# Fused memory-attention and gated feed-forward block on one core: an earlier first weight load, a reordered first copy, and a new table of priorities

## The chip, the cores and the metric

The kernel runs on one core of one Trainium2 chip. A core has five engines with a queue of their own each: TensorE (PE, matrix products into PSUM), VectorE (DVE), ScalarE (ACT), GpSimd (POOL) and SyncE (SP), which here issues every DMA transfer. The metric is the device time of one execution in microseconds, as the median of several runs.

## What is computed

The input is x, 2048 tokens by 1024 features in bf16. The reference computes

```
h   = x + A(layernorm(x))          # 32 heads of 32, four segments of 512 tokens
out = h + (silu(n @ w1) * (n @ w3)) @ w2     with n = layernorm(h), 3584 hidden features
```

A projects the normalised tokens with wq, wk and wv. In each of the four segments it runs causal softmax attention inside the segment, and adds what a running memory of the earlier segments returns for phi(q), mixed by a gate per head; the result is multiplied with wo. The change concerns the order of work only; what is computed stays as it is.

## The kernel before

**How it is built.** The Python program does not write the instruction streams by hand. Each step is an operation in a graph with its allowed engines, an estimated cost, what it reads and writes, a class `cls` and a sequence number. `Graph.schedule` then plays the graph through with these estimates: whenever an engine is free, it takes the ready operation with the lowest (class, sequence number). The order that comes out per engine is emitted, with semaphore waits for the dependences. So the order within each engine's queue is fixed before the program runs; if an estimate is off, the engine waits at that place for the real event, with everything behind it in the queue.

**The table SHIFT.** Operations are numbered in units (`stage()` starts a new one: one projection, one group of scores, one layer norm, one copy). For a unit that is in the table, `schedule` adds the first number to its sequence number and the second to its class:

```
late, cls = SHIFT.get(o.unit, (0, 0))
o.seq += late + 1e-6 * o.seq
o.cls += cls
```

The table therefore only says which of several ready operations goes first. It adds and removes no operation.

**The stages.** A layer norm and the q, k and v projections of a segment feed that segment's attention. In attention, for each of eight pairs of segment and half of the heads, there are ten groups of scores (line 1101, four PSUM banks each), each followed by an exponential on ACT (L1115) and a causal mask on POOL (L1124); then one long visit of products in columns of 32 (L1194 and its neighbours L1187 and L1029) for numerators, denominators and the memory. For segments 1 to 3 a visit that retrieves the memory (L1316) comes later. The denominators' reciprocals are spread over rows; for segments 2 and 3 this goes through DRAM: a store to `r_scr`, then eight loads with repetition (L1281) into `R0w` and `R1`. Between the visits the scheduler puts pieces of dense 128x128 products (all at L747): the next segment's projections, the product with wo, and, near the end, the first feed-forward products with w1 and w3. After about 400 us only the feed-forward part is left.

**The start.** `first_half` issues the loads in one queue: token tiles x0, x1, x2, then the first half of the first query weights (256 columns), tile x3, the first half of the key weights, and the remaining weights. The fourth item of each load is a scale for its estimated transfer time; it changes the schedule only. `first_tile` normalises tile t in place: statistics (tiles 0 and 2 on DVE, L874, L877, L900; tiles 1 and 3 on ACT, L860, L863), the power -1/2 on POOL (L901), two multiplications of 512 columns on DVE (L905), eight transposes on PE (L759) and two copies out of PSUM into `xnT`, each on DVE (L771) or ACT (L770), whichever the scheduler finds free. Statistics on DVE of tile 2 depend on `self.applied[0]`, the first multiplication of tile 0. The first projections (q and k, features 0 to 255) then run in pieces of 128 tokens, as soon as each tile is there.

Of the kernel before, what the change touches and what calls it, by code (L numbers as in the profile page):

```python
# [30 lines left out]
    0: (-18, 0), 3: (-173, 0), 4: (-182, 0), 5: (1074, 0), 6: (1041, 1), 7: (-959, -1),  # L31
    8: (-283, 1), 9: (1560, 1), 10: (-14, 0), 11: (1, 0), 12: (51, -1), 13: (-257, 0),
    14: (-1703, 0), 15: (2952, 0), 16: (-2912, 0), 18: (-87, -1), 19: (3455, 1), 20: (-401, -1),
    21: (22, 0), 22: (2924, -1), 23: (-669, 0), 24: (-328, -1), 26: (-261, -1), 27: (11, -1),
    28: (-153, 0), 29: (-317, 0), 31: (1524, -1), 32: (211, 0), 33: (-1, 0), 34: (2, 0),
    35: (-15, 0), 38: (118, 1), 39: (2057, 0), 40: (223, 0), 41: (2279, -1), 42: (914, 1),
    43: (-1135, 1), 44: (2665, 1), 45: (3218, 1), 47: (1997, 1), 48: (664, -1), 49: (1928, -1),
    50: (-2800, -1), 51: (7, 0), 52: (-1130, 0), 53: (116, 0), 54: (669, 0), 55: (1018, 0),
    56: (2, 0), 57: (-289, 1), 58: (4, 0), 59: (731, 0), 60: (-304, 0), 61: (-436, 0),
    62: (64, 1), 63: (-3, 0), 64: (-63, 0), 65: (-50, 0), 66: (-174, 0), 67: (-937, 0),  # L40
    68: (808, 0), 69: (1512, -1), 70: (28, 0), 71: (-58, 1), 72: (1441, 1), 73: (-75, 1),
    74: (2141, 0), 75: (778, 1), 76: (-752, 1), 77: (90, 1), 78: (-21, 0), 79: (151, 0),
    80: (1343, 0), 81: (-1130, 0), 83: (160, 0), 84: (687, 0), 85: (-676, 0), 86: (312, 0),
    87: (-266, 0), 88: (-263, 0), 89: (-1189, -1), 90: (-164, 0), 91: (680, 1), 92: (-1801, 0),
    93: (1499, 0), 94: (3153, 0), 95: (-261, 0), 96: (0, -1), 97: (-11, 0), 98: (2, 0),
    99: (944, 0), 100: (-54, 0), 101: (1016, 0), 102: (-842, 0), 103: (147, 0), 104: (-1191, 0),
    106: (-47, 0), 107: (121, 1), 108: (-1142, 0), 109: (-1295, -1), 111: (699, 0),
    112: (-365, -1), 113: (-594, 0), 115: (28, 0), 116: (2452, -1), 117: (-8, 0), 118: (676, 0),
    119: (54, 0), 120: (-1449, -1), 121: (235, 0), 122: (-9, -1), 123: (-13, 1), 124: (45, 0),
    125: (-1279, 1), 127: (-283, -1), 129: (555, 0), 130: (1438, -1), 132: (617, 1),  # L50
    133: (81, 0), 134: (-2285, -1), 135: (-179, 0), 136: (3199, 1), 137: (389, 0),
    138: (920, 0), 139: (146, 1), 140: (687, 1), 141: (27, 0), 142: (-619, 1), 143: (1934, 1),
    144: (-922, 0), 145: (415, -1), 146: (-312, 0), 147: (-26, 0), 148: (-870, 0),
    149: (2501, 1), 150: (1682, 0), 151: (-28, 0), 152: (609, 1), 153: (611, 0), 154: (-302, 0),
    156: (0, 1), 157: (-185, 1), 158: (391, 0), 159: (-373, 0), 160: (-610, 0), 161: (-1748, 0),
    162: (-133, 0), 163: (-4056, 1), 164: (1073, 1), 166: (-202, 0), 168: (-3204, -1),
    169: (-2075, -1), 170: (2581, -1), 171: (-39, 1), 172: (-122, 1), 173: (-18, 1),
    174: (-37, 0), 175: (34, 0), 176: (1853, 1), 177: (-140, 0), 178: (-301, 0), 179: (204, 0),
    181: (165, 0), 182: (-13, 0), 183: (-7, 0), 184: (687, -1), 185: (-271, 0), 186: (-861, 1),
    187: (-616, 1), 188: (355, -1), 189: (-1449, 1), 190: (1132, 0), 191: (114, 0),  # L60
    192: (-22, 0), 193: (-464, 0), 194: (-2, 0), 195: (294, 0), 196: (18, 0), 197: (-2089, 0),
    199: (-2443, 0), 200: (248, -1), 201: (1, 0), 203: (210, 1), 204: (-1070, 0), 206: (-70, 0),
    207: (1441, 0), 208: (525, 0), 209: (839, 0), 210: (10, 0), 211: (-262, 0), 212: (894, -1),
    213: (203, 1), 214: (-359, 1), 215: (-2, 0), 216: (696, -1), 217: (-735, 0), 218: (-51, 0),
    219: (4750, 0), 220: (-465, -1), 221: (-23, 0), 222: (-196, 1), 223: (399, 0),
    224: (-1932, 1), 225: (-192, 0), 226: (-134, 0), 227: (-1542, 1), 229: (153, 1),
    230: (-676, 1), 231: (-73, 0), 232: (618, 1), 234: (-465, 0), 235: (0, -1), 237: (222, -1),
    238: (609, 0), 239: (1282, 0), 241: (-183, 1), 242: (845, 1), 243: (811, -1),
    244: (1681, -1), 246: (6, 1), 248: (-2423, -1), 249: (11, 0), 250: (21, 0), 251: (-2902, 1),
    252: (-599, 1), 253: (927, 0), 255: (308, -1), 256: (4, -1), 257: (-382, 0), 258: (30, 0),  # L70
    259: (-35, 0), 260: (-73, -1), 261: (-386, 0), 262: (-58, 1), 263: (-1713, 0),
    264: (-165, 0), 265: (-369, 1), 266: (-12, 0), 267: (808, -1), 268: (1356, 0),
    269: (-538, 0), 270: (576, -1), 272: (27, 0), 273: (609, 0), 275: (-27, 0), 277: (0, -1),
    279: (-4, 0), 280: (-3, 0), 281: (176, 0), 282: (-28, -1), 284: (-175, -1),
    285: (-1255, -1), 286: (-196, 0), 287: (308, 0), 288: (1028, 0), 289: (-18, 0),
    290: (-217, -1), 291: (628, 0), 292: (21, 0), 293: (11, 0), 294: (1042, 0), 295: (6, 0),
    296: (150, -1), 297: (222, 0), 298: (1329, 0), 299: (-799, 0), 300: (-3, 0), 301: (303, -1),
    302: (-473, -1), 303: (2419, -1), 304: (528, 0), 305: (-99, 0), 306: (2531, -1),
    307: (-28, 0), 309: (-1338, 1), 310: (-4, 1), 311: (836, 0), 312: (-154, 0), 315: (-261, 0),
    316: (443, 0), 317: (-31, -1), 318: (-1464, -1), 319: (-220, 0), 320: (340, 0),  # L80
    321: (1268, 0), 322: (-21, -1), 323: (-2755, 1), 324: (-54, 0), 325: (1643, -1),
    326: (-57, 0), 327: (1851, 0), 328: (-2912, 0), 329: (317, 1), 330: (-690, 0),
    331: (-712, -1), 332: (-940, 0), 333: (-1099, 1), 334: (-615, 1), 335: (-16, 0),
    336: (496, 0), 337: (664, 0), 338: (-166, 0), 339: (-46, 0), 340: (-700, 0), 341: (-385, 1),
    342: (-1713, 0), 344: (51, 0), 345: (-756, -1), 346: (178, -1), 348: (803, 0),
    350: (1942, -1), 351: (169, 0), 352: (-492, 1), 354: (14, 0), 355: (-39, 0), 356: (290, 0),
    357: (99, 0), 358: (-389, 0), 359: (1761, 0), 361: (1409, 0), 362: (-58, -1), 363: (550, 1),
    364: (-95, 1), 365: (-140, 1), 366: (56, 1), 367: (-11, 1), 368: (-1627, 0),
    369: (-393, -1), 370: (-2089, 0), 372: (27, 0), 373: (204, -1), 374: (-55, 0),
    375: (-622, 0), 376: (-1005, -1), 377: (-179, 0), 378: (-1188, 1), 379: (1478, -1),  # L90
    380: (-865, -1), 381: (-543, 0), 382: (-70, 0), 383: (-64, 0), 384: (-1160, 0),
    385: (-2800, 0), 386: (0, 1), 387: (-193, 1), 388: (-133, 0), 390: (2419, 0),
    391: (2201, -1), 392: (-35, -1), 394: (45, -1), 395: (-2041, 0), 396: (410, 0),
    397: (571, 1), 399: (-543, -1), 400: (-965, 0), 401: (2531, 0), 402: (-462, -1),
    403: (-129, 0), 404: (-89, 1), 405: (-60, -1), 407: (-887, 1), 408: (3072, 0),
    409: (3013, 0), 410: (1761, 1), 411: (1584, 0), 413: (281, 1), 414: (562, 0),
    415: (-1293, -1), 416: (1707, 0), 417: (-995, -1), 418: (1637, 0), 419: (-785, -1),
    420: (3, 0), 422: (-913, -1), 423: (-121, -1), 424: (-7, 0), 426: (-2, 0), 427: (-1, 0),
    430: (-1, 0), 431: (14, 0), 432: (8, 0), 433: (-33, 0), 435: (-1086, 0), 436: (72, 0),
    437: (51, -1), 438: (-293, -1), 439: (37, 1), 440: (1527, 1), 441: (-212, 0),  # L100
    442: (-3190, 1), 443: (-1357, -1), 444: (-520, 1), 445: (904, 0), 446: (-1018, -1),
    447: (697, 0), 449: (2458, 0), 450: (-40, 0), 451: (-44, 0), 452: (-8, 0), 453: (-14, 0),
    454: (658, -1), 455: (-3, 0), 456: (1, 0), 457: (-3, 0), 459: (-2315, 1), 461: (-1, 0),
    462: (539, 0), 463: (66, 0), 464: (788, 1), 465: (29, 0), 466: (24, 0), 467: (2995, 0),
    468: (-306, 1), 469: (310, 0), 470: (-30, -1), 471: (-796, 0), 472: (-70, 1),
    473: (3455, 1), 474: (62, -1), 475: (-550, 0), 476: (-2089, 0), 477: (2158, 0),
    478: (-306, 1), 479: (4, 0), 480: (1506, -1), 481: (-470, -1), 482: (3857, 0),
# [500 lines left out]
class Kernel:  # L608
# [283 lines left out]
    def first_tile(self, t):  # L892

        x = self.xs[t][:, :]
# [8 lines left out]
        for b in range(2):  # L903
# [4 lines left out]
            gr = Group([(0,), (1,), (2,)], safe=True)  # L908
# [53 lines left out]
    def first_half(self):  # L962
# [16 lines left out]
        x = self.xnT[0]  # L979
# [531 lines left out]
```

The softmax here doesn't subtract the row's maximum and nothing guards it: scores larger than these inputs give would overflow.

## Time and profile before

| what | value |
|---|---|
| median of 3 runs | 888.77 us (888.38 to 888.92) |
| profiled execution | span 886.3 us |
| TensorE clock granted | 1.0 |
| busy: DVE, ACT, POOL | 449.2, 302.5, 178.4 us |
| HBM read, written | 84.94 MB, 9.44 MB |

In 40 slices the page shows where each engine is busy, in tenths of the slice (22 us each):

```profile
PE   9999999999999999999999999999999999999998
DVE  6697878786665797645545301323243333341011
ACT  5878675779645555511111000101011111110000
```

Read it as three stretches: the start, in which TensorE has little to do for some 8 us; attention with dense work between its visits up to about slice 17; and the feed-forward part, in which DVE and ACT have little to do. Matmuls are pipelined and the profile models their ends, so a 9 for PE does not say that no time is lost between them. The page's groups show the three largest rows, out and in by name, count, busy time and mean duration of one, and idle time before them:

```profile
L747 PE MATMUL ps<-hnT,w1b 128*128 128x512 bf16 x875 | 219.8, 379 | 2.0 <-issue 0.5
L747 PE MATMUL ps<-hnT,w3b 128*128 128x512 bf16 x879 | 217.1, 379 | 1.5 <-issue 0.5
L747 PE MATMUL ps<-w2b,hm 128*128 128x512 bf16 (+2 forms) x935 | 198.5, 366 | 0.9
```

### The profile page before, as it was taken

Reading aid. Unit: us, or ns where it says so; the run is one execution under the profiler, and the core shown is the slowest. Engines: PE = TensorE matmul, PEld = TensorE weight load, DVE = VectorE, ACT = ScalarE, POOL = GpSimd, SP = SyncE. Lnnn points to the kernel's source line nnn. Section 1 sums busy time; section 2 is a strip of 40 time slices with the busy share of each in tenths; the row PEclk is TensorE's granted clock in tenths of the full one; section 3 lists DMA queues with packets and bytes.
Section 4 is the critical chain, followed back from the end, with each engine's and each line's share of the span. In section 5 each row is a group of like instructions: output and inputs, shape, how many; then the busy total and the mean of one; then the engine's idle time right before and its main releaser. Section 6 shows DMA issues by size and latency. Waiting matters only on the chain.

```text
span 886.3 us, 13649 instructions
## 1 busy us (share of the span) xinstructions
PE 873.0 (99%) x5732; PEld 400.5 (45%) x5821; DVE 449.2 (51%) x699; ACT 302.5 (34%) x345; POOL 178.4 (20%) x226
## 2 busy tenths in 40 slices
PE   9999999999999999999999999999999999999998
PEld 5444444444444344444444444444444444444445
DVE  6697878786665797645545301323243333341011
ACT  5878675779645555511111000101011111110000
POOL 2544443455252455303000000000000000000000
PEclk9999999999999999999999999999999999999999
DMA  7869939464862736198354410221323321301010
GB/s 238 208 185 244 227 91 267 125 156 119 217 155 74 175 83 156 53 300 258 103 156 107 120 35 30 78 65 54 83 61 88 95 72 48 90 7 41 30 54 24
DMA packets 148796, 105.75 MB, mean 119 GB/s; under 512 B 46336, under 2 KB 134400, under 8 KB 147712
## 3 DMA queue, kind: packets, MB, share of 16 engines
q1 hardware_dynamic: 148736, 104.89, 44.5%
q8 instruction: 46, 0.75, 0.4%
q14 instruction: 14, 0.11, 0.0%
HBM read 84.94 MB, written 9.44 MB: 106 GB/s over the span
## 4 chain that ended last, share of the span: by engine, by line
PE 94%; DMA 2%; DVE 2%; issue 1%; POOL 0%; ACT 0%; SPq 0%; ACTq 0%; POOLq 0%; DVEq 0%
PE ps L747 88%; PE ps L1194 3%; PE ps L1101 3%; DMA R0w<-r_scr 1%; DMA r_scr<-T 1%; DVE oT L1332 0%; SPq L1281 0%; DMA xs<-in_A_x_dram 0%; PE ps L1029 0%; DVE lnst L874 0%; ACT et L1115 0%; PE ps L1316 0%; POOL et L1124 0%; DVE hm L1397 0%; PE ps L1187 0%
## 5 line engine op out<-in xcount | busy, mean ns | idle before, releaser
L747 PE MATMUL ps<-hnT,w1b 128*128 128x512 bf16 x875 | 219.8, 379 | 2.0 <-issue 0.5
L747 PE MATMUL ps<-hnT,w3b 128*128 128x512 bf16 x879 | 217.1, 379 | 1.5 <-issue 0.5
L747 PE MATMUL ps<-w2b,hm 128*128 128x512 bf16 (+2 forms) x935 | 198.5, 366 | 0.9
L1389 ACT ACTIVATE sg<-ps 128x512 bf16<-128x512 f32 x112 | 66.8, 597 | 385.9 <-PE ps L747 385.8
L1392 DVE SCALAR_TENSOR_TENSOR t<-sg,ps 128x512 bf16<-128x512 bf16 x112 | 76.7, 685 | 183.1 <-ACT sg L1389 182.6
L1115 ACT ACTIVATE et<-ps 128x2048 bf16<-128x2048 f32 x80 | 150.0, 1874 | 45.1 <-PE ps L1101 44.7
L747 PEld LDWEIGHTS ps<-w2b,hm 128*128 128x128 bf16 x952 | 90.9, 98 | 103.0
L747 PEld LDWEIGHTS ps<-hnT,w1b 128*128 128x128 bf16 x896 | 86.2, 98 | 106.3 <-issue 6.5
L747 PEld LDWEIGHTS ps<-hnT,w3b 128*128 128x128 bf16 x896 | 86.3, 98 | 106.1 <-issue 3.6
L1124 POOL TENSOR_SCALAR_AFFINE_SELECT et<-et 128x512 bf16<-128x512 bf16 (+1 forms) x96 | 93.1, 976 | 133.0 <-ACT et L1115 132.7
L1397 DVE SCALAR_TENSOR_TENSOR hm<-t,ps 128x512 bf16<-128x512 bf16 x112 | 76.2, 685 | 40.8 <-PE ps L747 39.0
L1421 DVE TENSOR_TENSOR ob<-hr,ps 128x512 bf16<-128x512 bf16 (+2 forms) x34 | 22.2, 655 | 120.6 <-PE ps L747 120.4
L747 PE MATMUL ps<-wo,oT 128*128 128x512 bf16 x246 | 60.9, 379 | 1.1 <-issue 0.8
L747 PE MATMUL ps<-xnT,wp 128*128 128x512 bf16 (+1 forms) x345 | 59.6, 320 | 1.3 <-issue 0.8
L747 PE MATMUL ps<-hnT,wp 128*128 128x512 bf16 x249 | 59.4, 380 | 0.8 <-issue 0.6
L1138 DVE TENSOR_TENSOR sum<-sum,et 128x512 bf16<-128x512 bf16 (+1 forms) x64 | 43.6, 684 | 11.6 <-POOL et L1124 6.1
L747 PEld LDWEIGHTS ps<-xnT,wp 128*128 128x128 bf16 x352 | 28.0, 98 | 26.9 <-issue 2.8
L747 PEld LDWEIGHTS ps<-wo,oT 128*128 128x128 bf16 x256 | 23.9, 98 | 29.9 <-issue 3.3
L747 PEld LDWEIGHTS ps<-hnT,wp 128*128 128x128 bf16 x256 | 23.5, 98 | 29.7 <-issue 3.9
L1101 PE MATMUL ps<-qT,kT 32*128 32x128 bf16 (+3 forms) x512 | 31.7, 301 | 0.0
L747 PE MATMUL ps<-wp,xnT 128*128 128x512 bf16 x123 | 30.2, 379 | 0.4 <-issue 0.2
L747 PE MATMUL ps<-wp,hnT 128*128 128x512 bf16 x123 | 29.6, 380 | 0.5 <-issue 0.3
(97 smaller groups left out, 560.1 us busy)
## 6 DMA issues: line engine op xcount, KB each, us to landing
w3b<-in_B_w_dram SPq DMA_DIRECT2D x28, 512.0 KB, 4.1
w1b<-in_B_w_dram SPq DMA_DIRECT2D x28, 512.0 KB, 4.0
wp<-in_A_wv_dram SPq DMA_DIRECT2D x8, 1024.0 KB, 6.5
wp<-in_A_wq_dram SPq DMA_DIRECT2D x7, 1024.0 KB, 5.6
wp<-in_A_wk_dram SPq DMA_DIRECT2D x7, 1024.0 KB, 7.2
w2b<-in_B_w_dram SPq DMA_DIRECT2D x7, 1024.0 KB, 5.8
xs<-in_A_x_dram SPq DMA_DIRECT2D x16, 256.0 KB, 5.9
h<-in_A_x_dram SPq DMA_DIRECT2D x16, 256.0 KB, 4.0
```

The source lines that it names most:

```text
L747: return [e.matmul(p[0](gr), p[1], p[2], start=p[3], stop=p[4]) for p in part]
L1101: ins.append(e.matmul(self.bank(gr, j, 512 - 128 * kc, off), k[r, g0 + g, 128 * kc:128 * kc + 128], q[r, g0 + g, 128 * kc:512], start=True ...
L1115: return [e.activation(et[:, :, :], src, AF.Exp, scale=self.scale)]
L1124: self.pool_op(lambda e, v=v, pat=pat: e.affine_select(v, v, pattern=pat, compare_op=ALU.is_ge, fill=0.0, base=0, channel_multiplier=-1), ...
L1138: lambda e, gr: [e.tensor_tensor(out, x, y, op=ALU.add)], reads=[x, y],
L1194: ins.append(e.matmul(self.ps[32 * i:32 * i + 32, b * 512 + c0:b * 512 + c0 + n], lhsT(i, kc, j), rhs(i, j), start=kc == 0 and j == first, ...
L1389: self.g.op("act", act_ns(512), lambda e, gr, sg=sg: [e.activation(sg, self.bank(gr), AF.Tanh, scale=0.5)], writes=[sg], cls=0, group=gg)
L1392: e.scalar_tensor_tensor(t1, sg, 1.0, self.bank(gr), op0=ALU.add, op1=ALU.mult)], reads=[sg], writes=[t1], cls=0,
L1397: e.scalar_tensor_tensor(dst, t1, 0.5, self.bank(gr), op0=ALU.mult, op1=ALU.mult)], reads=[t1], writes=[dst], cls=0,
L1421: self.g.op("dve", dve_ns(n), lambda e, gr, hs=hs, ob=ob, n=n: [e.tensor_tensor(ob, hs, self.bank(gr, 0, n), op=ALU.add)], reads=[hs], wri ...
```

## The change

Three edits. In the queue of loads, the first query weights go ahead of the third token tile x2, and the scales of these two loads are set anew. In `first_tile`, the first of the two copies of tile 0 may only run on DVE, and the statistics of tile 2 depend on that copy in place of the first multiplication, so that they come behind it. And the table SHIFT is replaced as a whole: nearly every entry has other numbers. The aim is that the first projection finds its weights and its tokens sooner, and that the rest of the schedule fits the new start.

```diff
 SHIFT = {
-    0: (-18, 0), 3: (-173, 0), 4: (-182, 0), 5: (1074, 0), 6: (1041, 1), 7: (-959, -1),
...
+    0: (-7, 0), 3: (38, 0), 4: (2985, 0), 5: (497, 1), 6: (310, 0), 7: (-6129, 0), 8: (-30, 1),
...
         var, mean, op = self.ln_act(t, x) if t % 2 else self.ln_stats(
-            t, x, 1, (self.applied[0],) if t else ())
+            t, x, 1, (self.copied,) if t else ())
...
-            self.evac(gr, out, 512, lambda v: v[:, 0:512].rearrange("p (k n) -> p k n", k=4),
-                      cls=1, bf=True, engs=("dve", "act"))
+            o = self.evac(gr, out, 512, lambda v: v[:, 0:512].rearrange("p (k n) -> p k n", k=4),
+                          cls=1, bf=True, engs=("dve", "act") if t or b else ("dve",))
+            if t == 0 and not b:
+                self.copied = o
...
-        loads = [x[0] + (1.04,), x[1] + (0.7,), x[2] + (1.2,),
-                 (wq[:, :, 0:256], sq[:, :, 0:256], 1.54), x[3] + (0.65,),
+        loads = [x[0] + (1.04,), x[1] + (0.7,), (wq[:, :, 0:256], sq[:, :, 0:256], 1.3),
+                 x[2] + (1.0,), x[3] + (0.65,),
                  (wk[:, :, 0:256], sk[:, :, 0:256], 0.74),
```

## The prediction

> **What bounds the kernel now.** I read the page's engine shares and its chain first, then the chain in order of time for the start, the timeline there, the waits of TensorE, and last a count of TensorE's visits. The page first:
>
> ```profile
> PE 873.0 (99%) x5732; PEld 400.5 (45%) x5821; DVE 449.2 (51%) x699; ACT 302.5 (34%) x345; POOL 178.4 (20%) x226
> ...
> PE 94%; DMA 2%; DVE 2%; issue 1%; POOL 0%; ACT 0%; SPq 0%; ACTq 0%; POOLq 0%; DVEq 0%
> ```
>
> TensorE is on 94% of the chain that ended last. The 99% alone prove little: one 512-column matmul is shown with 379 ns, but two that follow each other start 216 ns apart. So I counted weight loads between changes of kind in the trace. A dense stretch takes 216 ns for each load plus about 0.11 us: the chain below has 12 matmuls in 2.70 us, and 12 x 0.216 = 2.59. From the first projection to the end, TensorE makes 80 visits for scores, 8 for the columns, 6 for the retrieval and 4 groups of transposes, with a dense stretch between any two. The scores' visits take 0.33 us. Hardly a stretch is longer than its count. The exceptions in all of attention add up to 2.2 us: 0.9 at 298 us (the retrieval waits for rows of R), 0.5 at 309 (DVE hm), 0.35 at 266 (ACT sg), 0.3 at 175 (a mask) and 0.1 at 258. The view of TensorE's waits names the same places, with smaller sums because it counts from modelled ends:
>
> ```profile
> PE ps L1316 <- DMA R<-r_scr: 0.8, 1, 0.8
> PE ps L747 <- DVE hm L1397: 0.4, 1, 0.4
> PE ps L747 <- ACT xnT L770: 0.3, 1, 0.3
> PE ps L747 <- ACT sg L1389: 0.3, 1, 0.3
> ```
>
> So three things are left to win: these 2.2 us, the start, and the number of visits. The chain of the start, in order of time (start, duration, what):
>
> ```profile
> 6.07 0.47 DVE xs L905 x2
> 6.54 0.18 issue
> 6.72 0.69 DVE lnst L874
> 7.41 0.32 DVE xnT L771
> 7.73 0.30 DVE lnst L874
> 8.03 0.22 issue
> 8.25 0.72 DVE xs L905 x2
> ...
> 9.66 1.07 PE ps L747 x16
> 10.73 0.45 PE ps L759 x8
> 11.18 2.23 PE ps L747 x40
> 13.41 0.45 PE ps L759 x8
> 13.86 2.68 PE ps L747 x48
> ...
> 20.34 2.70 PE ps L747 x12
> ```
>
> VectorE leads until 9.66 us, TensorE from there without a gap: 40 small matmuls in 2.23 us are 56 ns each, the pitch at which they start one after another. The timeline shows what the first projection waits for:
>
> ```profile
> 7.05 0.60 ACT L770 ACTIVATE xnT<-ps 128x512 bf16<-128x512 bf16 x1
> 7.32 0.41 DVE L771 COPY xnT<-ps 128x512 bf16<-128x512 bf16 x1
> 7.76 0.68 PEld L747 LDWEIGHTS ps<-xnT,wp 128*128 128x128 bf16 x12 [0.62 <-DMA wp<-in_A_wq_dram]
> ```
>
> The copy by ACT ends at 7.65, and the weights, issued at 2.18 with 5.1 us to landing, are there at about 7.3. Both come close together, and the copy is the later.
>
> [...] x3, issued at 2.66, lands after 5.4 us at 8.1, and the key weights, issued at 3.81, after 6.7 us at 10.5. I use it for one thing: exchanging two loads leaves what lies behind both where it was.
>
> **The loads.** Before, x2 lands at about 5.6 us and wq at 7.3, in the trace's landing events. Exchanged, wq comes 256 KB earlier. x1 landed at 4.3, and wq took 7.3 - 5.6 = 1.7 us behind x2, so I expect it at 4.3 + 1.7 = 6.0 to 6.4; x2 then lands at about 7.3. x3 (8.1) and the key weights (10.5) have the same bytes ahead of them and stay.
>
> **The copy.** The first four transposes are done when ACT starts at 7.05. DVE needs 0.41 in place of 0.60, so the copy ends at 7.46 and the first projection starts at about 7.58 instead of 7.79: 0.2 us earlier. The second half goes to ACT (7.32 to about 7.92) or DVE (to 7.87). The eight matmuls on the first half last 8 x 56 ns = 0.45, to 8.03, so it is nearly in time: cost 0 to 0.1.
>
> **What queues behind the new wait.** On DVE, in order, behind the copy: the statistics of tile 2 (two of 0.69), the multiplications of tile 1 (0.72, ready at 7.94 when POOL ends), and the copies of tile 1. If the multiplications go first, they start at 7.97 and not 8.25, 0.3 earlier. If both statistics go first, they start at 7.46 + 2 x 0.69 = 8.84, 0.6 later. Tile 2 itself becomes ready 0.6 to 1.1 us later than its 10.67.
>
> **What reaches the end of the start.** Nothing, most likely. The key weights can be used from 10.5 to 10.6 us. At 10.57 TensorE has, before, just finished all it can do without key weights and tile 2: q for tiles 0 and 1. From there 96 matmuls and 16 transposes are left, 112 x 56 ns = 6.3 us, without a gap to 16.6. After the change the same work is left at the same time, since only tile 2 could be taken ahead and it comes later, not sooner. Its delay is hidden too: k for tiles 0 and 1 is 32 x 56 ns = 1.8 us, to 12.4, and tile 2 is multiplied by 11.8 at the latest. I take 0 for the start; the ends are -0.3 (if a few transposes slip in ahead) and +0.5 (if statistics go first, or a k matmul stands in the queue ahead of its weights).
>
> **The new table.** It adds no work. It can shift waits, and visits. The visits are forced: a score group needs four banks which ACT frees 1.88 us after the last one, so dense work has to lie between, and the columns and retrievals hold the same banks. 98 visits stay 98. What is left is the 2.2 us of waits. Nothing in the profile says that new priorities miss more or less often in the small; the largest wait, 0.9, is one of four retrievals fed through DRAM, of which the other three wait for nothing. I take 0.6 in its place: 2.2 becomes 1.9, from 0 to 6. That is the largest unknown. The scheduler's rate and fixed time for a load (260 bytes per ns and 1.9 us) give 2.9 us for the 256 KB store into r_scr; the chain at 286 us has 5.39. So the late retrievals are planned with a time that is too short, by luck of the table with slack or without. Sum: 0 for the start, -0.3 for waits: 888.77 - 0.3 = 888.5.
>
> **The rivals.** *Waits vanish.* All 2.2 us go, the start gives 0.1 to 0.3: 888.77 - 2.3 = 886.5 at the very best, typically 886.8. For it: TensorE needs nothing new, the five waits are separate, and the dense work is there to fill them. Against: the long ones depend on transfers whose time the schedule does not know. *A staged transfer is missed,* which ends slower. The loads of L1281 land in 3.2, 6.6 (median) and 10.1 us. A retrieval ordered for the median waits 10.1 - 6.6 = 3.5 us when it meets weight traffic, with all dense products queued behind it. There are four such retrievals, in segments 2 and 3; now one of them waits 0.9. One full miss gives 888.5 + 3.5 = 892.0, a partial one of 2 us or a few small ones 890.6 to 891. *The start turns against itself:* DVE takes both statistics first, and TensorE idles 0.5 us, 889.2. For it: tile 2's statistics are no longer done when tile 1 is ready. Against: the slack before the key weights.
>
> **How the numbers follow.** Likeliest, 50%: start hidden, waits of the same size, 888.5. Waits vanish, 20%: 886.8. A staged transfer missed, 22%: 891. Start against itself, 8%: 889.2. The bound of 0.2% is 1.8 us, so 887.0 and 890.5 are the limits: faster 0.2, same 0.58, slower 0.22. The range leaves out about half of each outer case: below 886.7 only nearly everything at once would do, above 891.3 a full miss.
>
> **What would show it.** The start: the first projection at about 7.6, but the first score visit still at 17.3 within 0.4. If it comes at 16.9 or earlier, the key weights landed sooner than I say, and my step on the loads is wrong. The visits: dense stretches of 216 ns per load plus 0.11, and 98 visits. The waits: the view of TensorE's waits with one to three entries of under 1 us. An entry of over 2 us at L1316 would be the staged transfer. If the time falls below 886.5, there was something left that my count of stretches did not see.

## The result, and the profile after

| | median us | range | ratio to before, 95% interval |
|---|---|---|---|
| before, beside it | 888.58 | 887.82 to 888.92 | |
| changed | 895.15 | 894.57 to 896.89 | 1.0078 (1.0061 to 1.0096) |

The change costs 6.6 us; the prediction said 888.5, with 891.3 as its upper end. The profiled execution of the changed kernel is its slowest, 896.89 us with a span of 895.2; the others are 1.2 to 2.3 us faster, and one reason for that comes out below. Line numbers in the changed kernel are 3 lower up to about L900 and 1 lower after it (L747 is L744, L1316 is L1315, L1281 is L1280). In most experiments the code is some 90 lines longer, so L744 is L834 to L839 there.

The page of the changed kernel, engine shares and chain:

```profile
PE 882.0 (99%) x5821; PEld 401.8 (45%) x5821; DVE 447.3 (50%) x699; ACT 301.5 (34%) x341; POOL 187.0 (21%) x230
...
PE 91%; DMA 5%; SPq 1%; DVE 1%; ACT 0%; issue 0%; POOL 0%; DVEq 0%
```

The busy shares have hardly moved: TensorE is at 99% as before. The chain has: TensorE fell from 94% to 91%, and transfers rose from 2% to 5%. The view of TensorE's waits names the places (engine, tile, line, releaser; then total us, times, longest):

```profile
PE ps L756 <- DVE xs L902: 2.3, 2, 1.3
PE ps L1315 <- DMA R<-r_scr: 1.6, 1, 1.6
PE ps L1028 <- issue: 1.3, 1, 1.3
PE ps L744 <- DVE oT L809: 1.2, 1, 1.2
PE ps L744 <- DMA h<-in_A_x_dram: 1.2, 1, 1.2
PE ps L1100 <- DVE R L1328: 0.9, 1, 0.9
PE ps L744 <- DMA w1b<-in_B_w_dram: 0.6, 1, 0.6
```

The idle 1.2 us ahead of the very first matmul (L809 here) were there before too. Beside them the kernel before had no wait with a named releaser over 0.8 us (under "issue", without a releaser, it had 3.7 us in 23 pieces of at most 0.2; its profile lacks the records of 89 of its 5821 matmuls). Now there are six entries from 0.6 to 2.3. To see where they lie I used the count of the prediction: the time from one kind of TensorE work to the next, less 0.216 us for each dense load (0.056 for each small piece), 0.106 for each return to dense work, 0.33 for a score visit, and for a column visit its columns at the pace of the dense loads, four products side by side (512 columns in 0.216 us; in the kernel before, four products of 256 columns start 0.11 us ahead of the next four). What is left, in us:

| stretch, us (rounded) | before | changed |
|---|---|---|
| start, to 22 | 0.6 | 3.7 |
| 22 to 170 | 1.1 | 1.6 |
| 170 to 245 | 1.1 | 2.2 |
| 245 to 262 | 0.1 | 1.5 |
| 262 to 330 | 2.3 | 2.7 |
| 330 to 375 | 0.1 | 1.6 |
| from 375 | 0.0 | 0.8 |
| sum | 5.2 | 14.1 |

The sums differ by 8.9 us, as the spans do (895.2 - 886.3): the loss is idle or slow time of TensorE, and two thirds of it lie behind the start. Of the 3.7 us at the start, 1.7 are lost to half clock, which only some executions have (below); in part that is why this slowest execution loses more than the 6.6 us of the medians. Dense stretches are 100 and column visits 10, against 98 and 8 before: the new order takes the first segment's columns in three parts.

### The profile page after: what moved, and what is told of

It reads as the page before. It is cut to its first block, busy times and chain, and to the rows that moved or that the text cites. A ratio compares the mean times of both kernels' runs of the same rounds, so it can differ in the third digit from the quotient of the medians.

```text
span 895.2 us, 13715 instructions
## 1 busy us (share of the span) xinstructions
PE 882.0 (99%) x5821; PEld 401.8 (45%) x5821; DVE 447.3 (50%) x699; ACT 301.5 (34%) x341; POOL 187.0 (21%) x230
## 4 chain that ended last, share of the span: by engine, by line
PE 91%; DMA 5%; SPq 1%; DVE 1%; ACT 0%; issue 0%; POOL 0%; DVEq 0%
PE ps L744 85%; PE ps L1193 3%; PE ps L1100 3%; DMA R0w<-r_scr 1%; DMA R<-r_scr 1%; DMA h<-in_A_x_dram 1%; DMA wp<-in_A_wk_dram 1%; SPq L1280 1%; DMA w1b<-in_B_w_dram 1%; ACT et L1114 0%; DMA r_scr<-T 0%; SPq L319 0%; POOL et L1123 0%; PE ps L1028 0%; DVE R L1328 0%
## 5 line engine op out<-in xcount | busy, mean ns | idle before, releaser
L744 PE MATMUL ps<-hnT,w1b 128*128 128x512 bf16 x896 | 221.4, 379 | 0.9 <-DMA w1b<-in_B_w_dram 0.6
L744 PE MATMUL ps<-hnT,w3b 128*128 128x512 bf16 x896 | 218.2, 379 | 0.0
L744 PE MATMUL ps<-w2b,hm 128*128 128x512 bf16 (+2 forms) x952 | 200.2, 366 | 0.0
L744 PEld LDWEIGHTS ps<-w2b,hm 128*128 128x128 bf16 x952 | 90.9, 98 | 103.0
L744 PEld LDWEIGHTS ps<-hnT,w3b 128*128 128x128 bf16 x896 | 86.5, 98 | 105.9 <-issue 2.9
L744 PEld LDWEIGHTS ps<-hnT,w1b 128*128 128x128 bf16 x896 | 86.1, 98 | 106.5 <-issue 7.0
L1123 POOL TENSOR_SCALAR_AFFINE_SELECT et<-et 128x512 bf16<-128x512 bf16 x96 | 95.3, 999 | 115.5 <-ACT et L1114 115.5
L744 PE MATMUL ps<-xnT,wp 128*128 128x512 bf16 (+1 forms) x352 | 63.3, 328 | 0.7 <-DMA wp<-in_A_wk_dram 0.5
L744 PE MATMUL ps<-wo,oT 128*128 128x512 bf16 x256 | 62.6, 380 | 1.2 <-DMA h<-in_A_x_dram 1.2
L744 PE MATMUL ps<-hnT,wp 128*128 128x512 bf16 x256 | 59.9, 380 | 0.0
L744 PEld LDWEIGHTS ps<-xnT,wp 128*128 128x128 bf16 x352 | 29.1, 102 | 27.2 <-issue 3.2
L744 PEld LDWEIGHTS ps<-wo,oT 128*128 128x128 bf16 x256 | 23.7, 98 | 31.4 <-issue 3.3
L1331 POOL TENSOR_TENSOR oT<-Nsb,R 128x512 bf16<-128x512 f32 x22 | 30.2, 1383 | 33.1 <-DVE R L1328 33.1
L744 PEld LDWEIGHTS ps<-hnT,wp 128*128 128x128 bf16 x256 | 23.5, 98 | 29.6 <-issue 3.8
L1137 DVE TENSOR_TENSOR sum<-et,et 128x1024 bf16<-128x1024 bf16 x32 | 28.7, 899 | 11.0 <-ACT et L1114 10.7
```

The costliest lines, as they stand in the source:

```text
L744: return [e.matmul(p[0](gr), p[1], p[2], start=p[3], stop=p[4]) for p in part]
L1123: self.pool_op(lambda e, v=v, pat=pat: e.affine_select(v, v, pattern=pat, compare_op=ALU.is_ge, fill=0.0, base=0, channel_multiplier=-1), ...
L1137: lambda e, gr: [e.tensor_tensor(out, x, y, op=ALU.add)], reads=[x, y],
L1331: self.either(lambda e, out=out, Ns=Ns, R1=R1: e.tensor_tensor(out, Ns, R1, op=ALU.add), 512, 2, [Ns, R1], [out], 2)
```

## The experiments

In all runs but the table alone and the changed kernel once more, every engine follows a recorded order of operations, the one of the kernel before, of the changed kernel, or of both in parts, and one or a few things in it are altered. Medians and ratios are against the kernel before on the same chip (888.4 to 889.0).

**The start alone, and the rest alone.** The first 104 operations are the start. One kernel takes the old start and the new order of all else, one the reverse; a third takes the old order with only the two loads exchanged.

```diff
-order: new start (loads x0 x1 wq x2 x3 ...), new rest
+order: old start (loads x0 x1 x2 wq x3 ...), new rest     # e1
+order: new start, old rest                                # e2
+order: old start with wq ahead of x2, old rest            # e3
```

> Every engine follows the order of the kernel before up to its last operation of the first 32 small projection pieces, and from there the order of the changed kernel. Theory (two parts that add): the start costs 2.6 us (the last small piece ends at 19.2 us after the change, 16.6 before), the new order of the rest the other 4.0 us of the 6.6; so this kernel takes 888.6 + 4.0 = 892.6. Rival 1, all in the start: 888.6. Rival 2, all in the new order of the rest: 895.2.

> The other graft: the start in the order of the changed kernel (loads exchanged, both statistics of tile 2 ahead of the multiplications of tile 1 on DVE), the rest in the order of the kernel before. Theory (two parts that add): 888.6 + 2.6 = 891.2. Rival 1, all in the start: 895.2. Rival 2, all in the rest, the later start hidden: 888.6.

> The kernel before with every engine's order as it was, but the first query weights issued ahead of the third token tile. On DVE the first statistics of tile 2 stand ahead of the second copy of tile 0, and the second ahead of the multiplications of tile 1. Theory: the exchange alone brings tile 2 to 8.1 us in place of 5.6 and the weights no sooner than 7.3; DVE stands until 8.1, tile 1 is multiplied at about 9.9 in place of 8.25, and the whole takes 888.6 + 1.0 to 2.6, say 890.4. Rival (what I predicted): the key weights, at 10.5, bound the start anyway, and the time stays at 888.6 within 0.5.

Measured: old start with new rest 896.12 (1.0090, 1.0069 to 1.0111); new start with old rest 889.63 (1.0009, 1.0002 to 1.0016); loads alone 890.47 (1.0019, 1.0012 to 1.0027). The new start by itself costs 0.6 us by the medians and 0.8 by the ratio. The rest by itself costs 7.1, as much as the whole change within the intervals. By the medians the two add up to more than the 6.6 us of the change; the intervals are too wide to prove that, but the timeline of TensorE in the kernel with the old start shows a loss that the changed kernel does not have:

```profile
13.53 2.84 PE L837 MATMUL ps<-xnT,wp 128*128 128x128 bf16 x48
17.94 0.81 PE L837 MATMUL ps<-wp,xnT 128*128 128x512 bf16 x3 [1.56 <-DMA wp<-in_A_wv_dram]
```

The new rest begins with a product of the values, whose weights land at 17.7 us. With the old start TensorE is there at 16.4 and waits 1.56 us. With the new start it comes to this product at 19.2 us in the first profile and at 17.6 in the second, and does not wait. So a later start hides this wait.

The new start with the old rest shows its own loss in its profile, which had the full clock: the first score visit comes 1.5 us later than the 17.33 of the profile before.

```profile
18.81 0.39 PE L1190 MATMUL ps<-qT,kT 32*128 32x512 bf16 x4
```

**The new table alone.** The old code with the new table, ordered by the scheduler itself.

```diff
-SHIFT = {0: (-18, 0), 3: (-173, 0), ...}
+SHIFT = {0: (-7, 0), 3: (38, 0), ...}
```

> The kernel before with the new table alone: old loads, old copy, and the planner orders the work itself. Theory (the table makes nearly all of the difference): 895 to 897, with R and wv among TensorE's waits. Rival (the table fits the changed start, and costs nothing or much more without it): the kernel is within 0.3% of before (below 891.5), or above 899.

Measured: 894.92 (1.0071, 1.0050 to 1.0092), which is 6.3 us. The table costs as much as the whole change without the other two edits.

**Tile 1 ahead of tile 2's statistics.** In the changed kernel VectorE stands idle from 7.2 to 8.1 us and then takes both statistics of tile 2 ahead of tile 1's multiplications, which had been ready at 7.7 (timeline of VectorE):

```profile
8.10 1.29 DVE L871 BATCH_NORM_STATS2 lnst<-xs 128x6 f32<-128x512 bf16 x2 [0.91 <-DMA xs<-in_A_x_dram]
9.30 0.40 DVE L902 TENSOR_SCALAR xs<-xs,lnst,rstd 128x512 bf16<-128x512 bf16 x1
```

```diff
-VectorE: copy, stats x2 a, stats x2 b, x1 a, x1 b, ...
+VectorE: copy, x1 a, x1 b, stats x2 a, stats x2 b, ...
```

> The changed kernel with one move: on DVE the two multiplications of tile 1 go ahead of both statistics of tile 2. Theory: in the changed kernel DVE stands from 7.2 to 8.1 us waiting for tile 2 while tile 1 has been ready since 7.7, and multiplies tile 1 at 9.3; with the move it does so at 7.8, TensorE does not wait 1.3 us for it, and the kernel gains 1.0 to 1.5 us: 893.9. Rival: TensorE then waits for the key weights at 10.6 instead and gains nothing: 895.1 within 0.4.

Measured: 895.27 (1.0075, 1.0063 to 1.0087), no gain. The wait of 1.3 us is gone, and this line stands in its place:

```profile
10.79 0.40 PE L834 MATMUL ps<-xnT,wp 128*128 128x128 bf16 x4 [1.87 <-DMA wp<-in_A_wk_dram]
```

TensorE now waits for the key weights, as the rival said. But they bind it only because of TensorE's own order, which this run leaves as it was: in the new order four products with the key weights stand ahead of the second half of tile 1's transposes and of all 16 q products of tile 1. The kernel before does these between 9.2 and 10.6 us, while the key weights are on their way. Putting them ahead on TensorE as well was not tried.

**The value product later.** In the kernel with the old start and the new rest, two products trade places.

```diff
-TensorE: small pieces, v product 0, ..., k product 3
+TensorE: small pieces, k product 3, ..., v product 0
```

> The kernel of the run with the old start and the new rest (896.1), with one change: the first product of the values and the second product of the keys trade places, on TensorE and on VectorE, so that the first product that needs the value weights comes at about 21 us and not at 13.5 us after the small pieces. Theory (the new table put a product that needs wv, which lands at 17.7, straight behind the start): the entry L744 <- DMA wv of 2.0 us goes, the time falls by 1.5 to 894.6. Rival (the second key weights or the copies behind them become the wait, or the loss reappears at the score visits): 895.6 to 896.1.

Measured: 895.29 (1.0069, 1.0053 to 1.0085), 0.8 us less than without the exchange. In the view of waits the two entries for wv, 2.0 us together, fall to 0.6, as the theory said. Of these 1.4 us only 0.8 are in the time, and the intervals of the two runs overlap: the wait is shown, its full price is not.

**The rows R.** The retrieval at 347 us waits for four loads from `r_scr` (trace of the changed kernel: the issues on SyncE, then the matmul):

```profile
335.47 1.73 SPq L1280 DMA_DIRECT2D R0w<-r_scr  x4
337.24 1.81 SPq L1280 DMA_DIRECT2D R<-r_scr  x4
347.50 0.44 PE L1315 MATMUL ps<-pq,Mbf 32*32 32x512 bf16 x16 [1.58 <-DMA R<-r_scr]
```

The kernel before issues them the other way round:

```profile
334.16 1.72 SPq L1281 DMA_DIRECT2D R<-r_scr  x4
335.92 1.82 SPq L1281 DMA_DIRECT2D R0w<-r_scr  x4
343.52 0.43 PE L1316 MATMUL ps<-pq,Mbf 32*32 32x512 bf16 x16
```

First experiment: turn the rows round, with what consumes R0w later on VectorE and GpSimd.

```diff
-SyncE: R0w x4, R x4        VectorE: Nsb j=1 early
+SyncE: R x4, R0w x4        VectorE: Nsb j=1 behind the first products with R
```

> The changed kernel, every engine in its recorded order, but in segment 3 the four loads of the R rows (L1280) are issued ahead of the four loads for R0w, as in the kernel before, and the five products that need R0w stand later on VectorE and GpSimd. Theory (the retrieval at 347 us waits 1.6 to 2 us because its rows stand behind four other loads in the ring): the entry L1315 <- DMA R falls below 0.3, and the time by 1.6 to 2.0, to 893.4. Rival 1 (the wait only moves: the late R0w products now hold up VectorE's copies behind the retrieval, and TensorE waits for those instead): about 1 us of waits on DVE at 345 to 355, time 894.6. Rival 2 (the landing does not depend on the place in the ring, but on all traffic of that stretch): R lands as late as now, 895.1 or above.

Measured: 895.35 (1.0071, 1.0052 to 1.0089). The retrieval now runs at 341.93 without a wait, and some seven microseconds later TensorE waits for VectorE, behind the very product that was moved (timelines of VectorE and TensorE):

```profile
347.73 1.75 DVE L1385 TENSOR_TENSOR Nsb<-Nsb,R0w 128x512 f32<-128x512 f32 x1
350.22 1.02 PE L834 MATMUL ps<-hnT,w3b 128*128 128x512 bf16 x4 [1.71 <-DVE t L1481]
```

The wait moved into the queue that I had changed for it. This shows that the repair was bad, not that R is free. So the second experiment moves nothing and makes the R0w loads small:

```diff
-to, src = R0w rows, 2048 elements
+to, src = to[:, 0:512], 512 elements      # these four loads only
```

> The changed kernel in its recorded order; in segment 3, first half, the four loads for R0w move a quarter of their bytes (the three other quarters of R0w aren't loaded, their products use the first quarter, so this part of the output is wrong). Nothing is reordered. Theory (the retrieval at 347 us waits 1.6 to 2 us because R stands behind 1 MB of other rows): R lands at least 1.5 us sooner after its issue, the entry L1315 <- DMA R falls below 0.4, and the time by 1.2 to 1.8, to 893.6. Rival (VectorE and GpSimd, whose queues are full there, take the wait over, as the entry DVE t 1.7 did when the R rows went first): 0 to 0.5 less.

Measured: 892.38 (1.0052, 1.0038 to 1.0066), against 895.49 (1.0085, 1.0072 to 1.0099) for the changed kernel beside it: 3.1 us less, where 1.2 to 1.8 had been expected. In executions at full mean clock alone the difference is about 3 us too (medians 892.04 and 895.27); why it is more than the wait of 1.6 to 2.2 us is not shown. The landing of the four R loads, in us from issue, minimum, median, maximum, in the changed kernel and then with the small R0w loads:

```profile
DMA to landing us min/median/max: 6.8/7.9/8.6
```

```profile
DMA to landing us min/median/max: 3.3/4.5/5.5
```

In the kernel before, with R ahead, they take 3.2 to 5.6, and in the run with the R rows first 4.6 to 7.0. So the wait comes from the place in the queue: R landed 3 us sooner as soon as the 1 MB ahead of it was a quarter, and the entry of TensorE for it was gone.

**The gap at 252 us.** It is 1.46 us, within a hundredth, in every profile with the new rest up to here, so a transfer is not likely behind it: wq, for one, landed anywhere from 7.3 to 8.5 us in the seven profiles without the exchange. TensorE and VectorE in the changed kernel:

```profile
252.08 0.43 PE L1315 MATMUL ps<-pq,Mbf 32*32 32x512 bf16 x16
252.44 1.90 PE L744 MATMUL ps<-hnT,w1b 128*128 128x512 bf16 x8
254.63 1.90 PE L744 MATMUL ps<-wp,xnT 128*128 128x512 bf16 x8 [0.28 <-DMA wp<-in_A_wv_dram]
257.47 0.40 PE L1100 MATMUL ps<-qT,kT 32*128 32x128 bf16 x8 [0.94 <-DVE R L1328]
```

```profile
252.73 0.75 DVE L1328 SCALAR_TENSOR_TENSOR R<-ps,gcol,R 128x512 f32<-128x512 f32 x1 [1.06 <-PE ps L1315]
253.40 0.42 DVE L1002 TENSOR_SCALAR pq<-qT 128x1024 bf16<-128x1024 bf16 x1
253.73 0.74 DVE L1328 SCALAR_TENSOR_TENSOR R<-ps,gcol,R 128x512 f32<-128x512 f32 x1
254.40 1.10 DVE L1004 TENSOR_TENSOR pq<-pq,phe 128x1024 bf16<-128x1024 bf16 x1
...
256.67 0.74 DVE L1328 SCALAR_TENSOR_TENSOR R<-ps,gcol,R 128x512 f32<-128x512 f32 x1
```

Two waits share the gap. First suspect: the value weights.

```diff
-dma(wv second half, 8 chunks)
+dma(wv second half, chunk 0)      # this one load only
```

> The changed kernel in its recorded order, with one load cut: of the second half of the value weights in segment 3 (1 MB, issued at 243 us and landed at 254.6) only the first of eight chunks is loaded; the products use what else lies in the buffer, so these values are wrong. Theory (TensorE's 1.46 us without work at 252 to 255 us waits for this load, which the new order issues 17 us later because its buffer comes free later): the gap falls below 0.4, the time by 1.0 to 1.4, to 894.0. Rival (the score banks, held by VectorE's products with R at the same place, take over): the gap stays above 1.0 and the time within 0.4 of the changed kernel run beside it.

Measured: 895.04 (1.0073, 1.0061 to 1.0085), 0.4 under the changed kernel beside it, within the intervals. The rival was right, and one pair of lines says it:

```profile
252.42 1.89 PE L836 MATMUL ps<-wp,xnT 128*128 128x512 bf16 x8
255.71 0.40 PE L1192 MATMUL ps<-qT,kT 32*128 32x128 bf16 x8 [1.40 <-DVE R L1420]
```

The wait for the weights is gone, and the score visit waits 1.40 instead of 0.94: the stretch behind the retrieval lasts 5.02 us as before. A retrieval fills four banks; VectorE empties them in four products with R, the last of which ends 5 us after the retrieval; the new order puts only 16 matmuls (16 x 0.216 + 0.106 = 3.56 us) between it and the next scores. In the kernel before VectorE is no faster there. Its four products stand among the same instructions, and the last of them too ends 5 us after the retrieval. But the old order has 24 weight loads there (24 x 0.216 + 0.106 = 5.29 us), and 24 to 32 behind each of its other retrievals that scores follow:

```profile
253.19 0.43 PE L1316 MATMUL ps<-pq,Mbf 32*32 32x512 bf16 x16
253.55 0.55 PEld L747 LDWEIGHTS ps<-hnT,w3b 128*128 128x128 bf16 x4 [0.23 <-issue]
254.22 3.33 PEld L747 LDWEIGHTS ps<-hnT,w1b 128*128 128x128 bf16 x16
257.79 0.74 DVE L1329 SCALAR_TENSOR_TENSOR R<-ps,gcol,R 128x512 f32<-128x512 f32 x1
257.98 0.56 PEld L747 LDWEIGHTS ps<-hnT,w3b 128*128 128x128 bf16 x4 [0.43 <-ACT phe L722]
258.97 0.40 PE L1101 MATMUL ps<-qT,kT 32*128 32x128 bf16 x8
```

The next run makes two of VectorE's instructions between the four products small.

```diff
-tensor_scalar(pq, ...), tensor_tensor(pq, ...)      128x1024
+tensor_scalar(pq part, ...), tensor_tensor(...)     128x128   # these two only
```

> The changed kernel in its recorded order; two of VectorE's instructions that stand between its four products with R at 252 to 257 us, a copy (0.42 us) and a multiplication-sized minimum (1.10 us) for pq, work on an eighth of their columns (this part of pq is wrong). Nothing is moved. Theory (the score visit waits until VectorE has freed the four banks of the retrieval, and 16 matmuls are too few to cover that): the entry L1100 <- DVE R falls to 0, the stretch of 5.02 us behind the retrieval shortens to 3.6 to 4.1 (the value weights can hold it for 0.4), the time by about 1.0 against the changed kernel's 895.3, to 894.3. Rival (the gap is a lack of dense work and reappears at the next score visit): the stretch shortens, but a new gap of about 1 us stands before the next visits, and the time is within 0.3 of 895.3.

Measured: 894.43 (1.0065, 1.0051 to 1.0080). The stretch behind the retrieval falls from 5.02 to 4.45 us, by 0.6 and not by 1.0, and the wait for R does not fall to 0 but to 0.8: the two small instructions still take 0.18 and 0.73 us in place of 0.42 and 1.10, and the four products and what else stands between them fill the rest. No new gap appears behind it. So the scores wait until VectorE has freed the banks; that the time falls with it is not shown by this run alone, as its interval overlaps that of the changed kernel.

**Do the causes add?** Three kernels with the old start and the new rest, with more and more repairs:

```diff
+v product later, R rows first                              # e8
+v product later, R0w and wv loads cut                      # e11
+v product later, R0w and wv loads cut, two pq cut          # e14
```

> The old start and the new rest with both repairs: the R rows first and the value product later. Theory (two separate waits, which add): 896.1 - 1.5 - 1.7 = 892.9. If the R wait only moves, 894.2. If the two are not what sets the time: above 895.5. Nothing expects before's 888.9: the stretches at 250 us and 376 us and the two additional visits are left.

> The old start with the new rest, the value product later, and both loads cut as in the two runs before (the same two parts of the output are wrong). Theory (separate waits that add: 1.5 at the start, 1.2 at 250, 1.5 at 347): 896.1 - 4.2 = 891.9, which leaves about 3 us over the kernel before for the two additional visits, 375 us, and many small ones. If the waits replace each other: above 893.5.

> The run with the value product later and both loads cut (892.9), and in addition the two pq instructions cut (three parts of the output wrong). Theory (the gap behind the retrieval at 252 us is a loss of its own): 892.9 - 1.3 = 891.6. Rival (it reappears behind): 892.6 to 893.0. Left over the kernel before would be about 3 us: waits for h at 188 us, for w3b at 376 us, the column visits, two more visits.

Measured: 893.93 (1.0055, 1.0042 to 1.0069), 892.91 (1.0055, 1.0043 to 1.0067) and 891.26 (1.0033, 1.0021 to 1.0045), from 896.12. The medians fall with each repair, 4.9 us in all. The first two sums fell short by about 1 us (892.9 and 891.9 had been expected); in the first the wait of 1.3 us for VectorE is still there. The last step, 1.65 us, is a little more than expected. So the losses add in the main, and none of them stands for all. What is left over the kernel before on the same chip, 2.8 us, was not tried; the last profile shows waits in it of 1.3 us in the column visit at 274 us (a stall in which the profile shows no releaser), 0.8 at 254 (R), 0.6 for w3b and 0.5 at 189 us (h).

**The changed kernel once more,** for its spread.

> The changed kernel itself once more, as the measure for the three others on this chip, and for its spread: 895.0 within 0.7 on the median. In the first profile of it TensorE was granted half its clock from 11 to 14.4 us. If that is not the rule but a matter of single executions, the profile of this run shows 1.00 there with two chances in three, and the first score visit at 19.2 and not at 21.0 us.

Measured: 895.49 (893.95 to 897.62). As expected, the clock at the start is 1.00 in this profile, and the first score visit comes at 19.5 us. The time from 335 to 360 us in its profile holds more than the R wait:

```profile
345.80 0.44 PE L1315 MATMUL ps<-pq,Mbf 32*32 32x512 bf16 x16 [2.18 <-DMA R<-r_scr]
346.18 1.58 PE L744 MATMUL ps<-hnT,w3b 128*128 128x512 bf16 x4
347.55 1.91 PE L744 MATMUL ps<-hnT,w1b 128*128 128x512 bf16 x4
349.26 1.37 PE L744 MATMUL ps<-hnT,w3b 128*128 128x512 bf16 x4
```

Behind the wait, the next group of four matmuls starts 1.4 and 1.7 us after the last one, where it is 0.86 from 350.46 us on, at full clock. The granted clock from 345 to 350 us is 0.66 in the mean, 1.00 in the 5 us on both sides; the 1.71 us from 347.55 to 349.26 are twice 0.86, the pace of half the clock. The first profile of the changed kernel has the same at the start, where the wait was (windows of 1 us: length, PE busy, granted clock, DMA share, GB/s):

```profile
10.00:11.00 1.00, 0.52 (x8) 0.88 1.02 253
11.00:12.00 1.00, 1.00 (x12) 0.50 1.07 300
12.00:13.00 1.00, 1.00 (x13) 0.50 1.06 320
13.00:14.00 1.00, 1.00 (x12) 0.50 1.05 339
14.00:15.00 1.00, 1.00 (x19) 0.91 1.06 339
```

The lost clock adds up to 0.12 + 3 x 0.5 + 0.09 = 1.71 us, which is 3.4 us at half clock. With one such stretch the mean clock of the whole execution is 0.998 in both profiles. With the loads alone exchanged, 7 of 18 executions have this mean (median 891.92; the other 11: 889.81); of the kernel before, 2 of 97, over five chips. It is not the whole spread: the slowest execution of the changed kernel here, 897.62, has a mean of 1.000. The last experiment tests whether TensorE's idle time brings it on.

```diff
 TensorE: first 8 small pieces
+         4 matmuls of 512 columns into an unused bank
          4 small pieces
+         2 matmuls of 512 columns into an unused bank
```

> The kernel before with the loads alone exchanged (890.47 with 7 of its 18 executions at a mean clock of 0.998), and in addition six 512-column matmuls into an unused bank, four behind the first eight small pieces (8.5 to 9.6 us) and two behind the next four (about 10 us), where TensorE stood idle. Theory (idle time in the first 11 us brings on the half clock): no execution, or at most one, below 1.000, and the median falls to that of the undisturbed executions, 889.9. Rival (the half clock comes by chance, whatever TensorE does): a third of the executions stays at 0.998, and the time at 890.5 or a little above, for the six additional matmuls.

Measured: 889.51 (1.0007, 1.0000 to 1.0013), and of 21 executions none below 1.000. By the medians, six matmuls that nobody reads win 1 us here, and with TensorE's idle time filled no execution shows the half clock. Two reserves: this run and the one with the loads alone were on different chips, and their intervals touch; and in the profile of this run wq landed at 6.34 us, against 7.87 there, so some of the idle time was gone without the six. How often that was so is not known. No kernel of the study is faster than the kernel before; this one and the new start with the old rest come closest.

## Why the prediction was wrong, point by point

- **The loads: wrong in size.** In the first profile wq landed at 7.39 us, where 6.0 to 6.4 had been said, against 7.32 in the kernel before. But landings differ from execution to execution, and the prediction took its figures from one profile, in which wq happened to land earliest of all without the exchange. Over the profiles of all runs the median for wq is 7.5 with the exchange (6.3 to 7.9, ten profiles) and 8.0 without (7.3 to 8.5, seven): 0.5 us sooner, where 0.9 to 1.3 had been said. x2 pays for it with 2.6 us (8.2 against 5.6; 1.7 had been said). The step took a landing as bytes ahead over a rate. What lies behind both was to stay, my estimate from the order of the landings in that one profile, and nearly did: x3 has 8.9 against 8.7, the key weights 9.8 to 11.0 in four profiles against 10.46 in one.
- **The copy: right.** It took 0.42 us, to 7.19, and the first projection started at 7.43 (said: 7.58), but it waited for the weights and not for the copy.
- **The queue behind it: the worse branch, and worse than said.** The statistics went first, as one of two ways. Tile 1 was multiplied 1.05 us later than before, not 0.6, since x2 was late.
- **The start hidden behind the key weights: wrong in its reason, small in size.** The first score visit was to stay at 17.3 within 0.4. With the new start and the old rest it came at 18.81, at full clock. "The same work is left" when the key weights land was false: TensorE's new order has key products ahead of q for tile 1, so 16 products and 4 transposes more were left, 20 x 56 ns = 1.1 us. The prediction had named this branch (a k matmul in the queue ahead of its weights) and given it +0.5. (Eight of the 112 pieces of its sum come behind the first score visit, so that 6.3 us do not end at the 16.6 it gives.) By the medians the start costs less than the 1.5 us between the two profiles, of which that of the kernel before had early landings: 889.4 for the executions at full mean clock, against 889.0. Moving tile 1 ahead on VectorE alone won nothing. The half clock, in 3 of 21 executions there, was left out.
- **The visits: wrong by two.** 98 visits were called forced. The column visit can be cut, and was cut in three; by the measured 0.106 us for a return to dense work that is a few tenths.
- **The new table: the step that failed.** "2.2 becomes 1.9, from 0 to 6." Measured: 6.3 us for the table alone; in the table of stretches above, what is lost behind the start grows from 4.6 to 10.4 us, 5.8 more where the prediction took 0.3 less. (The 2.2 were the larger exceptions alone.) The argument priced one kind of wait, the staged transfer. It gave a miss 2 to 3.5 us, and making the loads ahead small won 3; but it looked for the cause in weight traffic, and what R stood behind were the other 1 MB of rows in its own queue. All other waits it treated as small because the old order had none. An order also settles which load meets which product (values at 16.4 us, when wv lands at 17.7), how many matmuls cover VectorE's work on four banks (16, where the old order has 24), and in which order eight loads share a queue. The old order was right in each of these; nothing says that another one is. The sum over such places was the missing term.

Of the rivals, the missed transfer came true, with more behind it. Its sign in the prediction was an entry of over 2 us at L1316; it showed with 1.6 in the first profile and 2.2 in the second. One full miss alone was to give 892.0; the time lies another 3 us above.

## What to carry to other kernels

A new table of priorities is a new program, even when no operation is added: forecast it from the number of places where an engine's queue, a bank or a transfer is only just in time, not from the waits that the old order happens to have. When a repair is tried, prefer one that takes the suspected load or work away over one that moves it: the move of R came back as a wait of VectorE, while making the loads ahead of it small showed 3 us. Before calling an engine too slow, look at the same place in the kernel before: VectorE took the same 5 us there, and the order had enough matmuls to cover them. And look at the granted clock behind an idle stretch of TensorE: behind the wait of 2.18 us here another 1.7 us were lost.

## What the hardware showed beyond that

A wait of TensorE was followed by a loss of clock, which cost nearly as much again. After 2.18 us of idle time at 343.6 to 345.8 us, in the second profile of the changed kernel, the granted clock was 0.66 in the mean of the 5 us from 345 us on, a loss of 1.7 us. After a start in which TensorE was busy half of the time from 7 to 11 us (0.76, 0.50, 0.24 and 0.52 of each microsecond), in the first profile, it was 0.50 in each microsecond from 11 to 14 us, and the loss was 1.7 us too. If the clock was half throughout, each loss stands for about 3.4 us, an estimate from these two sums. Executions with a mean clock below 1.000 were 7 of 18 with the loads alone exchanged and 3 of 21 with the new start and the old rest. A start that was busy for hardly more of these 4 us (0.84, 0.65, 0.10 and 0.52 of each, in the profile of the new start with the old rest) kept a clock of 1.00. What decides between the two was not shown.
